# Chunk-selected attention feeding a softplus FFN: another start, a causal triangle by matmul, and a new order of all instructions

## The chip, the cores and the metric

The kernel runs on one core of one Trainium2 chip. The metric is the device time in microseconds of one execution. Engines are called by the profile's names: PE (TensorE, with PEld for its weight loads), DVE (VectorE), ACT (ScalarE), POOL (GpSimd) and SP (SyncE, which here only issues DMAs).

## The reference

q, k and v have 4 batches, 8 heads, 768 positions and 64 dimensions in f32. Each row of 768 keys is cut into 24 chunks of 32. For each query and chunk, an upper bound of the score is formed from the chunk's minimum and maximum of k; the six chunks with the highest bounds are kept, with a causal limit by chunk. Attention then runs over the kept chunks with the ordinary causal mask, and its output, 3072 tokens by 512, goes through an FFN with softplus.

```python
k_min = np.min(k_chunks, axis=3); k_max = np.max(k_chunks, axis=3)
ub = np.sum(np.maximum(q * k_min, q * k_max), axis=-1)      # per query and chunk
ub = np.where(causal, ub, -1e9)
top_chunks = np.argsort(ub, axis=-1)[..., -6:]
mask = (key's chunk is in top_chunks) & (pos[:, None] >= pos[None, :])
attn = softmax(np.where(mask, q @ k.T / 8, -1e9))
x = attn @ v                                                 # 3072 x 512
h = x @ w_in                                                 # 512 -> 2048
out = softplus(h) @ w_out                                    # 2048 -> 512
```

## The kernel before, in words

The work is cut into twelve blocks of 256 queries (4 batches of 3); block n is batch n // 3 and stretch n % 3. A block attends to the keys of its own stretch and of the earlier ones of its batch. Its four head pairs are handled one after the other.

For one block the steps are, by the names that the plan uses:

- Loads. `load` (line 330) issues two DMAs on POOL's queue for k, q or v, which turn f32 into bf16 on the way (line 339). k and q of block 0 come instead by `load_pairs` (line 345): four f32 halves on SP's queue into `xp` (line 352), each then cast into `io` by ACT or DVE. The FFN weights come in four chunks each on POOL's queue (`w_in`, line 376; `w_out`, line 383).
- k and q are transposed: by PE in blocks 0 to 2 (line 471), by a DMA transpose on SP's queue from block 3 on (line 475).
- DVE reduces k by chunk to maximum and negated minimum (`kx`, `kn`, lines 490 and 498) and copies them into a block-diagonal tile (`bd`). q is copied and split into its positive and negative part (`qc`, `qpn`, lines 547 to 551). PE forms the bounds (`ub`, line 570; line 574 adds the causal limit in blocks 0 to 2).
- DVE finds the sixth largest bound (`mx`, `raw`, lines 582 to 615). The mask, 32 rows a head, is transposed (`mT`, lines 627 and 633, or a DMA at line 636) and copied below q in the tiles `qa` and `qt` (`mc`). Block 0 does all this in two groups of two head pairs, the other blocks in one.
- The scores (`s`, lines 687 and 688) are one matmul over 96 or 128 rows: 64 of k and q, and 32 more, in which q's side holds the mask and k's side (`KA`, `KB`) holds one-hot rows that say to which chunk a key belongs and carry a large negative number. So a key of a chunk that is not selected gets a score that exp turns into 0.
- ACT takes exp into `pt` (line 695). In the two key tiles on the diagonal POOL then zeroes what lies above it (`af`, `affine_select`, line 705). PE multiplies by v with a column of ones (`av`, line 717), DVE divides (`nm`, lines 727 and 728), and the result is transposed into X (line 743 by PE and a copy in blocks 0 to 2 and the last; line 732 by DMA in the others).
- The FFN: `h` (line 791), exp (line 796) and ln(1 + x) (line 801) on ACT, `y` (line 816), a copy out of PSUM (line 822) and a store on SP's queue (line 827).

The one-hot rows are built in `ohb`: DVE fills it (line 270, one instruction for all three stretches), POOL cuts each stretch with three selects (lines 275 to 279), and SP's queue spreads them over the head pairs (`rows_of`, line 305), first the stretch of block 0, then the two others. Batches 1 and 3 use a second set of tiles, whose rows, like the loads of block 3, are gated on the last chunk of w_out.

None of this order is written out. `make_plan` lists operations with their engines (several where there is a choice), estimated costs, dependences and a key, a time by which they are wanted; `Plan.run` (line 136) passes urgencies back along the dependences and places one operation after the other by earliest start and urgency, with a model of the DMA queues (lines 179 to 188). The engines then run exactly in that order. All keys come from `PAR` (line 224): `a` holds the start of each block's scores, `prep` the lead of its preparation, `hlag` and `ylag` the lag of its FFN, `ahead` and `loads` the loads, `sizes` the number of buffers of each kind.

```python
o.due = min([o.key] + [s.due - dur for s in o.succ])          # line 146
lim = min(x[0] for x in v) + tol.get(e, 0)                    # line 169
x = min((x for x in v if x[0] <= lim), key=lambda x: (x[1].due, x[0], x[1].n))
```

At last `keep_awake` (line 837) fills the gaps that the plan leaves on PE in the first 45 us with matmuls of a zero tile (line 852). Their product is read by nobody.

Of the kernel before, what the change touches and what calls it, by code (L numbers as in the profile page):

```python
# [12 lines left out]
ALU = mybir.AluOpType  # L13
# [50 lines left out]

class Op:
    __slots__ = ("name", "alts", "fn", "deps", "gate", "after", "succ", "alloc", "touch", "key",
                 "rel", "packet", "port", "due", "wait", "eng", "start", "end", "done", "dma", "n", "at", "inst")


class Plan:  # L70
# [5 lines left out]
    def op(self, name, alts, fn, deps=(), alloc=(), touch=(), key=None, dma=None, gate=(), after=(), rel=0.0, packet=19.0, port=False):  # L76
        o = Op()
        o.rel, o.packet, o.port = round(rel), packet, port
# [50 lines left out]
    @staticmethod  # L129
    def home_at(pool, s, e):  # L130
        t = 0.0
        for q, x, dma in pool.ends[s]:
            t = max(t, x + (LANDED[e] if dma else 0 if q == e == "PE" else LAT[q].get(e, 150)))
        return t

    def run(self, par):
# [11 lines left out]
        ring, packet = {"SP": 0.0, "POOL": 0.0}, {"SP": 19.0, "POOL": 32.0}  # L148
# [3 lines left out]
        while ready:  # L152
# [26 lines left out]
            if o.dma:  # L179
                other = "SP" if e == "POOL" else "POOL"  # L180
                at = max(o.end + (650 if e == "SP" else 1150), ring[e], 2650.0)
                back, part = max(0.0, ring[other] - at), packet[other] / o.packet
                ring[e] = at + o.dma + min(o.dma * part, back)
                ring[other] += min(o.dma, back / part)
                packet[e] = o.packet
                o.done = ring[e] + (450 if o.packet < 100 else 1000)
                if e == "SP":
                    o.end = max(o.end, ring[e] - 3500)
            else:
                o.done = o.end  # L190
# [4 lines left out]
            for b in o.touch:  # L195
                b.left -= 1
                b.ends.append((e, o.done, bool(o.dma)))
# [22 lines left out]
def dve(n, rate=1.0):  # L220
    return n / (0.96 * rate) + 66


PAR = dict(
    dmat=3,
    dmaT=450,
    narrow=1,
    l0=1,
    over="soy",
    maskD=3,  # L230
    awake=(1.06, 45.0, 5.7),
    first=(64.42, 64.23, 29.03, 95.39),
    loads=((87.43, 130.15, 71.7), 19.14, (76.86, 12.06, 15.17), 41.22),
    tol={"PE": 0, "ACT": 0, "DVE": 0, "POOL": 2358, "SP": 0},
    alt=636,
    ohd=(229.35, 150.58),
    a=(-46.8, -33.92, -31.03, -0.05, 17.1, 24.77, 54.71, 88.7, 133.12, 175.62, 173.66, 255.42, 297.45, 469.8),
    prep=((77.31, -48.97, -81.43, 46.38), (-8.14, 24.92, -67.86, -43.68), (53.78, -16.07, -58.0, 11.26), (25.03, -41.37, -16.45, 11.23)),
    av=(-0.8, 4.76),
    ot=(12.12, 10.86),  # L240
    hlag=(8.7, 27.7, 34.1, -3.53, 34.9, 33.84, 33.54, 32.2, 25.36, -32.32, 54.03, 77.81),
    ylag=(7.32, 7.87, 25.64, 26.35, 28.67, 47.05, 47.88, 49.45, 10.02, 22.03, 47.36, 37.39),
    ahead=(3.4, 19.67, 10.64, 22.05, 12.72, 9.33, 70.63, 47.4, 103.95),
    sizes=dict(s=2, h=2, y=1, o=1, t=2, xf=2, xp=4, kT=2, io=8, kx=2, q=2, pn=2, ub=2, pt=4, osb=4, x=4, g=2, e=4, ysb=4, mT=2),
# [3 lines left out]
def make_plan(T, par):  # L248
# [19 lines left out]
    P.op("zero", [("DVE", 80)], lambda e: nc.vector.memset(T.zero, 0.0), key=-100000)  # L268
    ident = P.op("ident", [("POOL", 520)], lambda e: make_identity(nc, T.ident), key=1000)
    ohm = P.op("ohm", [("DVE", 700)], lambda e: nc.vector.memset(T.ohb, NEG), key=900)  # L270
    oh = []
    for k in range(NBLK):
# [8 lines left out]
        oh.append(P.op("oh", [("POOL", 1330)], f, [ohm], key=1500 + 6000 * k))  # L281
# [13 lines left out]
    chunk_rows = [P.op("c4", [("POOL", 900)], f4, [r4], key=3000)]  # L295
    mr0, bd0, kb0, vone, ohk = [], [], [], [], {}
# [11 lines left out]
    for k0, k1 in ((0, 1), (1, NBLK)):  # L308
        for h in range(2):
            o = P.op("ohk", [("SP", 450)], lambda e, k0=k0, k1=k1, h=h: rows_of(0, k0, k1, h), oh[k0:k1],  # L310
                     key=par["ohd"][k0] * 1e3, dma=300 * (k1 - k0))
            for k in range(k0, k1):
                ohk[0, k, h] = o
# [14 lines left out]
    def load(nm, n, when, gate=()):  # L328
# [6 lines left out]
        for t in range(NT):  # L335
# [4 lines left out]
                     gate=gate, key=key, rel=key - 2000 if n > 2 else 0.0, dma=950 if n < 3 else 2050, packet=32.0, **new)  # L340
            first = first or o
            ld[nm, n, t] = o

    def load_pairs(nm, n, when):
# [4 lines left out]
        for g in range(2):  # L349
# [4 lines left out]
                     key=1e3 * when[g], dma=950, packet=29.0, alloc=[st])  # L354
# [6 lines left out]
    def load_rows(nm, n, when):  # L361

        for t in range(NT):
            st = Buf(pool["xf"])
            d = P.op(f"ld {nm}{n}.{t}", [("SP", 560)], lambda e, t=t, st=st: nc.sync.dma_start(out=st.ap, in_=rows(nm, n, t)),
                     key=1e3 * (when + 0.3 * t), dma=1000, alloc=[st])
# [5 lines left out]
    def load_w_in(when):  # L372
        for c in range(4):
# [4 lines left out]
            w_in.append(P.op(f"w_in{c}", [("POOL", 800)], f, key=1e3 * (when + 0.4 * c), dma=2550, packet=173.0, after=w_in[-1:]))  # L378

    def load_w_out(when):  # L380
        for c in range(4):
# [4 lines left out]
            w_out.append(P.op(f"w_out{c}", [("POOL", 800)], f, key=1e3 * (when + 0.4 * c), dma=2550, packet=173.0,  # L386
# [5 lines left out]
    load_pairs("k", 0, (0.0, l0[0]))  # L392
    if par["l0"] < 2:
        load_pairs("q", 0, (l0[1], l0[2]))
    else:
        load("q", 0, l0[1])
# [4 lines left out]
    for nm, x in zip("kqv", l1):  # L401
        load(nm, 1, x)
    load_w_in(li)
    for nm, x in zip("kqv", l2):
        load(nm, 2, x)
    load_w_out(lo)
    for h in range(2):
        o = P.op("ohk", [("SP", 450)], lambda e, h=h: rows_of(1, 0, NBLK, h), oh, gate=[w_out[3]], key=40000, dma=900)
# [539 lines left out]
```

## Time and profile before

| | |
|---|---|
| three runs | 264.69, 266.26, 267.5 us; median 266.26 |
| the profiled execution | 266.59 us, of which the span of the trace is 264.8 us |
| granted PE clock over the span | 0.994 |
| busy | PE 255.0, PEld 197.2, DVE 142.5, ACT 211.0, POOL 110.8 us |
| line 852, the filler | 243 matmuls, 22.7 us of PE's 255.0 |
| longest line | 791, 91.8 us |
| DMA | 29.87 MB moved, 113 GB/s on average |

The page gives busy time by engine and in 40 slices of the span, the chain of work that ended last, and groups of instructions with their mean duration and the idle time ahead of them. Answers of the trace give the same for any stretch ("busy time by stretches": stretch, length, then busy time and number of instructions of PE, PEld, DVE, ACT and POOL, then the granted clock, the DMA share and GB/s) or for one line alone, and list instructions in order of time (start, duration, engine, line, operation, and in brackets how long the engine sat idle before it and what released it). Matmuls overlap in the pipeline, so that the sum of durations of a short one says less than the step from one start to the next.

### The profile page before, as it was taken

How to read it: one execution, taken by the hardware profiler on the slowest of the kernel's cores; microseconds unless marked ns; L12 is line 12 of the kernel's file. 1: busy time of each engine (PE TensorE's matmuls, PEld its weight loads, DVE VectorE, ACT ScalarE, POOL GpSimd, SP SyncE). 2: the span in 40 equal slices, each digit the busy share in tenths (PEclk: the TensorE clock that was granted, in tenths of full speed). 3: DMA queues.
4: the chain of work that ended last, by engine and by line, in shares of the span. 5: the costliest groups of instructions: out<-in, count | busy, mean ns of one | idle time of the engine just before them, and what ended most of it. 6: DMA issues, size and time to landing. Idle time of an engine off the chain costs nothing.

```text
span 264.8 us, 7039 instructions
## 1 busy us (share of the span) xinstructions
PE 255.0 (96%) x2750; PEld 197.2 (74%) x2779; DVE 142.5 (54%) x500; ACT 211.0 (80%) x372; POOL 110.8 (42%) x193
## 2 busy tenths in 40 slices
PE   8698999999999999999999999999999999999995
PEld 8698898768775677788678864777888756887744
DVE  6589961019789667447634596584582164221012
ACT  3589999988687879999687992699997885999900
POOL 8927878798318520543990263401110211310000
PEclk9799999999999999999999999999999999999999
DMA  7996999999999984699699969624440123001022
GB/s 162 161 189 90 181 196 231 155 139 190 149 136 173 132 119 89 115 129 100 73 173 150 117 88 174 173 54 120 45 82 0 42 72 99 10 2 42 0 79 79
DMA packets 114719, 29.87 MB, mean 113 GB/s; under 512 B 104544, under 2 KB 111712, under 8 KB 114688
## 3 DMA queue, kind: packets, MB, share of 16 engines
q0 software_dynamic: 74944, 13.11, 66.5%
q1 hardware_dynamic: 39744, 16.33, 33.0%
q8 instruction: 21, 0.34, 0.6%
q14 instruction: 10, 0.08, 0.1%
HBM read 27.26 MB, written 6.29 MB: 127 GB/s over the span
## 4 chain that ended last, share of the span: by engine, by line
PE 86%; DMA 5%; DVE 3%; ACT 3%; issue 1%; POOL 0%; DVEq 0%; POOLq 0%
PE ph L791 30%; PE py L816 17%; PE pt L816 9%; PE po L717 7%; PE ps L687 5%; PE py L852 4%; PE ps L688 4%; DMA io<-in_k_dram 3%; DMA x<-osb 3%; PE pt L687 2%; PE pt L688 1%; PE pt L570 1%; ACT g L801 1%; PE ph L816 1%; ACT e L796 1%
## 5 line engine op out<-in xcount | busy, mean ns | idle before, releaser
L791 PE MATMUL ph<-x,w_in_sb 128*128 128x256 bf16 x768 | 91.8, 272 | 0.0
L705 POOL TENSOR_SCALAR_AFFINE_SELECT pt<-pt 128x256 bf16<-128x256 bf16 x96 | 39.5, 419 | 112.6 <-ACT pt L695 112.1
L791 PEld LDWEIGHTS <-w_in_sb 128*128 128x128 bf16 x768 | 73.6, 98 | 11.5 <-DMA w_in_sb<-in_moe_w_in_dram 0.5
L695 ACT ACTIVATE pt<-ps 128x512 bf16<-128x512 f32 (+1 forms) x134 | 69.9, 564 | 9.4 <-PE ps L688 8.8
L796 ACT ACTIVATE e<-ph 128x512 f32<-128x512 f32 x96 | 56.3, 606 | 12.5 <-PE ph L791 11.8
L816 PEld LDWEIGHTS <-g 128*128 128x128 bf16 x400 | 37.4, 98 | 31.4 <-ACT g L801 0.5
L816 PE MATMUL py<-w_out_sb,g 128*128 128x512 bf16 x231 | 57.8, 379 | 1.5 <-ACT ysb L258 0.2
L801 ACT ACTIVATE g<-e 128x1024 bf16<-128x1024 f32 x48 | 51.1, 1072 | 1.0
L695 ACT ACTIVATE pt<-pt 128x512 bf16<-128x512 f32 (+1 forms) x58 | 32.4, 584 | 0.6 <-PE pt L688 0.6
L717 PEld LDWEIGHTS <-pt 128*128 128x128 bf16 x672 | 26.8, 97 | 5.1 <-issue 0.6
L259 DVE COPY ysb<-py 128x512 f32<-128x512 f32 x12 | 8.3, 691 | 36.9 <-PE py L816 36.9
L717 PE MATMUL po<-v,pt 128*128 128x65 bf16 x610 | 26.4, 193 | 0.3 <-DVE osb L728 0.3
L816 PE MATMUL pt<-w_out_sb,g 128*128 128x512 bf16 x108 | 26.2, 379 | 0.2
L727 DVE RECIPROCAL rec<-po 128x4 f32<-128x4 f32 x43 | 7.6, 178 | 34.9 <-PE po L717 34.6
L490 DVE TENSOR_REDUCE kx<-kT 128x32 bf16<-128x1024 bf16 x18 | 21.0, 1209 | 8.9 <-DMA kT<-io 8.9
L852 PE MATMUL py<-zero 128*128 128x128 bf16 x243 | 22.7, 245 | 1.1 <-DVE zero L268 1.1
L339 POOL DMA_DIRECT2D v<-in_v_dram x24 | 21.6, 905 | 3.8 <-DMA io<-in_q_dram 1.5
L339 POOL DMA_DIRECT2D io<-in_k_dram x22 | 20.0, 910 | 5.7 <-DMA w_in_sb<-in_moe_w_in_dram 2.2
L339 POOL DMA_DIRECT2D io<-in_q_dram x22 | 19.9, 910 | 0.7 <-PE ph L791 0.6
L728 DVE TENSOR_TENSOR osb<-po,rec 128x256 bf16<-128x256 f32 x43 | 18.2, 424 | 2.7 <-DMA x<-osb 1.3
L852 PEld LDWEIGHTS <-zero 128*128 128x128 bf16 x243 | 18.3, 111 | 1.3 <-DVE zero L268 1.1
L687 PE MATMUL ps<-qa,ka 96*128 96x256 bf16 x71 | 18.3, 273 | 0.7 <-DVE qa L259 0.7
(99 smaller groups left out, 302.5 us busy)
## 6 DMA issues: line engine op xcount, KB each, us to landing
out_dram<-ysb SPq DMA_DIRECT2D x23, 256.0 KB, 2.4
v<-in_v_dram POOLq DMA_DIRECT2D x24, 128.0 KB, 7.6
io<-in_k_dram POOLq DMA_DIRECT2D x22, 128.0 KB, 7.2
io<-in_q_dram POOLq DMA_DIRECT2D x22, 128.0 KB, 7.1
w_out_sb<-in_moe_w_out_dram POOLq DMA_DIRECT2D x4, 512.0 KB, 8.0
w_in_sb<-in_moe_w_in_dram POOLq DMA_DIRECT2D x4, 512.0 KB, 9.6
xp<-in_k_dram SPq DMA_DIRECT2D x2, 256.0 KB, 3.2
xp<-in_q_dram SPq DMA_DIRECT2D x2, 256.0 KB, 6.3
```

The source lines that it names most:

```text
L339: lambda e, t=t: nc.gpsimd.dma_start(out=into(nm, n, t), in_=rows(nm, n, t)),
L490: nc.vector.tensor_reduce(kx.ap[:, :, j].rearrange("d p (t c) -> d t p c", t=NT), kT.ap.rearrange("d p x -> d (p x)").rearrange("d (t p c ...
L687: nc.tensor.matmul(sp.ap[:, 0:QB], kk[0:nr, p, j * 128:(j + 1) * 128], qq, start=True, stop=True)
L695: lambda e, sp=sp, pt=pt, h=h, j=j, w=w: nc.scalar.activation(pt.ap[:, h, j:j + 2].rearrange("k j c -> k (j c)")[:, 0:w], sp.ap[:, 0:w], A ...
L705: nc.gpsimd.affine_select(out=d, in_=d, compare_op=ALU.is_ge, fill=0.0, base=0, channel_multiplier=-1, pattern=[[0, 2], [1, 128]])
L717: nc.tensor.matmul(o[:, u, h], pt.ap[:, h, j, c0:c0 + 128], T.V[i][:, j, 2 * p + h, :], start=(j == 0), stop=(j == t0 + u))
L728: nc.vector.tensor_tensor(osb.ap[0], o[:, :, :, 0:D], osb.ap[1].to_broadcast([128, NT, 2, D]), op=ALU.mult)
L791: nc.tensor.matmul(o[:, j], T.w_in[:, dt, ft * 128:(ft + 1) * 128], x.ap[:, dt], start=(dt == 0), stop=(dt == KDM - 1))
L796: lambda e, hb=hb, eb=eb, f2=f2: nc.scalar.activation(eb.ap[:, f2 * 512:(f2 + 1) * 512], hb.ap, ACT.Exp),
L801: lambda e, eb=eb, g=g, f4=f4: nc.scalar.activation(g.ap[:, f4 * 4:(f4 + 1) * 4].rearrange("f j c -> f (j c)"), eb.ap, ACT.Ln, bias=1.0),
L816: nc.tensor.matmul(yb.ap[:, 0:c1 - c0], g.ap[:, f, u * 128:(u + 1) * 128], T.w_out[:, f, c0:c1], start=(f == 0), stop=(f == KFF - 1))
L852: z.fn = lambda e: T.nc.tensor.matmul(T.pools["y"].homes[0][:, 0:128], T.zero, T.zero, start=True, stop=True)
```

## The change

The parts, and the diff cut to them:

- The fill of `ohb` is split, and the stretch of block 0 with its three selects has the most urgent key of all. The DMAs that spread these rows stand on SP's queue behind the four f32 halves. Loads on POOL's queue do not start before 3.3 us.
- The keys of all blocks are new. Block 0's scores lead block 1's by 29.7 us of key (12.9 before). In `first`, the halves of k and q of block 0 have new keys, k ahead.
- In blocks 0 and 1 the causal triangle is no longer cut by POOL out of `pt`. A tile `tri` holds 0 where a key may be seen and the large negative number where not; each score matmul on the diagonal leaves its accumulation open, and a matmul of `ident` and `tri` over 128 columns adds it.
- The planner's DMA model is replaced (class `Rings`: two queues that take turns, with a cost by packet, a time to land, and seven transfers at most on POOL's queue), all DMA costs are new, each operation's urgency can be moved by name (`tweak`, some 250 numbers), and the buffers change: io 8 to 7, q 2 to 3, pt 4 to 5, ysb 4 to 2.
- The filler matmuls have 512 columns where the gap allows it, 128 otherwise; the zero tile is 512 wide.
- `load_both` and the parameters `both` and `whole` are new, but with both=0 and l0=1 they are not used.

```diff
-        free = {"PE": 3000.0, ...}; ring, packet = ...
+        for o in topo:
+            o.due += 1e3 * par["tweak"].get(o.name, 0.0)
+        rings = Rings()
...
-    loads=((87.43, 130.15, 71.7), 19.14, (76.86, 12.06, 15.17), 41.22),
-    a=(-46.8, -33.92, -31.03, -0.05, 17.1, 24.77, 54.71, 88.7, 133.12, 175.62, 173.66, 255.42, 297.45, 469.8),
-    sizes=dict(..., io=8, kx=2, q=2, pn=2, ub=2, pt=4, osb=4, x=4, g=2, e=4, ysb=4, mT=2),
+    loads=((163.59, 151.05, 84.9), 87.8, (77.28, 67.14, 224.83), 15.3),
+    a=(-78.8, -49.07, -44.44, -42.37, 34.33, 59.68, 104.86, 105.55, 175.21, 244.28, 267.91, 364.15, 491.78, 674.36),
+    sizes=dict(..., io=7, kx=2, q=3, pn=2, ub=2, pt=5, osb=4, x=4, g=2, e=4, ysb=2, mT=2),
+    tweak={"w_out1": 39.87, "ld q0": 2.76, ...},
...
-    ohm = P.op("ohm", [("DVE", 700)], lambda e: nc.vector.memset(T.ohb, NEG), key=900)
+    ohm = [P.op(f"ohm{j}", [("DVE", 270 + 200 * j)], lambda e, j=j: nc.vector.memset(
+        T.ohb[:, QB:] if j else T.ohb[:, 0:QB], NEG), key=-900000 + 902000 * j) for j in range(2)]
...
-        oh.append(P.op("oh", [("POOL", 1330)], f, [ohm], key=1500 + 6000 * k))
+        oh.append(P.op(f"oh{k}", [("POOL", 1330)], f, [ohm[min(k, 1)]], key=1500 + 6000 * k if k else -900000))
...
+        t0_ = P.op("tri0", [("DVE", 100)], lambda e: nc.vector.memset(T.tri, 0.0), key=2000)
+        tri_ = [P.op("tri", [("POOL", 430)], lambda e: nc.gpsimd.affine_select(
+            out=T.tri, in_=T.tri, compare_op=ALU.is_ge, fill=NEG, base=0, channel_multiplier=-1, pattern=[[1, 128]]), [t0_], key=8000), ident]
...
-                     key=par["ohd"][k0] * 1e3, dma=300 * (k1 - k0))
+                     key=par["ohd"][k0] * 1e3 if k0 else -90000, dma=280 * (k1 - k0), packet=35.0 * (k1 - k0), land=2500.0 if k0 else 1000.0)
...
-  gate=gate, key=key, rel=key - 2000 if n > 2 else 0.0, dma=950 if n < 3 else 2050, packet=32.0, **new)
+  gate=gate, key=key, rel=key - 2000 if n > 2 else 3300.0 if par["l0"] == 1 else 0.0, dma=850, packet=13.3, land=(...), **new)
...
+                        add = last and tri
+                        for c0, c1, x in ((0, QB, qq), (QB, w, qq[:, 1] if last else qq)):
+                            jj = j + c0 // QB
+                            nc.tensor.matmul(sp.ap[:, c0:c1], kk[0:nr, p, jj * 128:(jj + 1) * 128], x, start=True, stop=not add)
+                            if add:
+                                nc.tensor.matmul(sp.ap[:, c0:c0 + 128], T.ident, T.tri, start=False, stop=True)
...
-                    if last:
+                    if last and not tri:
...
+        for w in (512, 128):
+            while True:
+                c = w / 1.2 if t < 1e3 * par["awake"][2] else mm(w)
```

More of the change, by code (lines that the diff above doesn't have):

```diff
@@ L179, in run @@
             if o.dma:
[L180 to L186, printed above, removed]
+                for x, y in rings.add(o, t - 2500.0):
+                    y += x.land
+                    if x is o or x.done != y:
+                        x.done = y
+                        for z in x.succ:
+                            z.at.clear()
                 if e == "SP":
-                    o.end = max(o.end, ring[e] - 3500)
+                    o.end = max(o.end, o.done - o.land - 3500)
             else:
@@ L238 @@
[L238 to L244, printed above, removed]
+    awake=(1.14, 45.0, 5.7),
@@ L837, in keep_awake @@
 def keep_awake(T, order, par):
-    fill, free = [], 1e3 * par["awake"][0]
+    fill, free = [], max(1e3 * par["awake"][0], 140 + next(o.end for o in order if o.name == "zero"))
     for o in order:
```

208 lines of the change are left out of this document (151 added, 57 removed).

## The prediction, made before the changed kernel ran

> **What bounds the kernel now.** I read the page first, then the busy time by stretches, then the same stretches for the filler matmuls alone (line 852, whose product nobody reads), then the timeline of the front, engine by engine.
>
> ```profile
> span 264.8 us, 7039 instructions
> ...
> PE 255.0 (96%) x2750; PEld 197.2 (74%) x2779; DVE 142.5 (54%) x500; ACT 211.0 (80%) x372; POOL 110.8 (42%) x193
> ```
>
> TensorE is busy 96% of the span, but part of that is filler. The next two answers separate it; each row is a stretch, its length, and busy time by engine (the second answer holds line 852 alone).
>
> ```profile
> 0.00:21.00 21.00, 17.61 (x228) 16.65 (x229) 14.97 (x43) 13.16 (x20) 15.23 (x31) 0.92 1.49 167
> 0.00:28.00 28.00, 23.90 (x347) 22.56 (x348) 21.64 (x73) 19.69 (x31) 20.86 (x41) 0.94 1.32 151
> 0.00:36.00 36.00, 31.48 (x476) 29.24 (x476) 29.14 (x106) 27.47 (x47) 27.32 (x53) 0.95 1.32 158
> ```
>
> ```profile
> 0.00:21.00 21.00, 13.83 (x140) 11.72 (x141) 0.92 1.49 167
> 0.00:28.00 28.00, 18.42 (x201) 15.36 (x201) 0.94 1.32 151
> 0.00:36.00 36.00, 21.51 (x234) 17.54 (x234) 0.95 1.32 158
> ```
>
> ```profile
> 60.00:240.00 180.00, 178.26 (x1900) 135.09 (x1923) 105.57 (x376) 149.89 (x270) 63.17 (x112) 1.00 0.93 103
> ```
>
> In the first 36 us TensorE does 31.48 - 21.51 = 9.97 us of work that counts, so 26.03 us are lost there. From 60 to 240 us it is busy 178.26 of 180: 1.74 us are left to win. The front is the only place where this change can gain much, and the long middle can almost only lose.
>
> What ends the front is the first FFN matmul (line 791), since FFN work is what keeps TensorE full afterwards. It needs X of block 0 and the first chunk of w_in.
>
> ```profile
> 36.06 1.03 PE L791 MATMUL ph<-x,w_in_sb 128*128 128x256 bf16 x8
> ```
>
> ```profile
> 34.64 0.64 ACT L258 COPY x<-pt 128x256 bf16<-128x256 bf16 x2
> ```
>
> I read the copies ending at 35.28 as the last of block 0's X, 0.8 us ahead of 36.06; call 36.06 T0. The question is how far T0 comes forward. For a T0 of 28 the same working gives a loss of 28 - (23.90 - 18.42) = 22.52 us, and for 21 it gives 21 - (17.61 - 13.83) = 17.22. So 8 us of T0 are worth 3.5 us: the work that was done before T0 must then be done behind it.
>
> **The change, part by part.** *One-hot rows.* Now they go out from 9.81 on, and the first lands 5.6 us later.
>
> ```profile
> ka<-ohb SPq DMA_DIRECT2D x1, 64.0 KB, 5.6
> ```
>
> ```profile
> 9.81 0.75 SPq L307 DMA_DIRECT2D ka<-ohb  x1
> ```
>
> ```profile
> 17.41 0.57 ACT L258 COPY qa<-ph 32x512 bf16<-32x512 bf16 x1
> ```
>
> ```profile
> 18.04 0.27 PE L687 MATMUL ps<-qa,ka 96*128 96x256 bf16 x1
> ...
> 18.20 0.27 PE L687 MATMUL ps<-qa,ka 96*128 96x256 bf16 x1
> ```
>
> The first of the two has landed at 15.4. The first scores start at 18.04, right behind the mask copy that ends at 17.98. So the rows are not the last to come, and moving them alone is worth 0. They become necessary once the mask is earlier: sent at about 4 and as slow as now they land near 10, soon enough for a mask at 10 or later. The moved selects (about 1.3 us on POOL) now stand ahead of the identity, which then is there at about 3.3 us; block 0's first k half is cast only at 4.46 (3.84 + 0.62, below), which hides it, and each us beyond that would be paid in full. On SP the rows stand behind the four halves, and nothing of the front is queued behind them there.
>
> *POOL's loads held until 3.3 us.* The q halves arrive late today because POOL's loads run beside them.
>
> ```profile
> 3.84 0.62 ACT L258 CAST io<-xp 128x512 bf16<-128x512 f32 x1 [1.75 <-DMA xp<-in_k_dram]
> 4.72 0.62 ACT L258 CAST io<-xp 128x512 bf16<-128x512 f32 x1 [0.26 <-DMA xp<-in_k_dram]
> 7.67 0.62 ACT L258 CAST io<-xp 128x512 bf16<-128x512 f32 x1 [2.33 <-DMA xp<-in_q_dram]
> ```
>
> ```profile
> 10.64 0.62 ACT L258 CAST io<-xp 128x512 bf16<-128x512 f32 x1
> ```
>
> ```profile
> 2.08 1.90 POOL L339 DMA_DIRECT2D io<-in_k_dram  x2
> ```
>
> ```profile
> DMA to landing us min/median/max: 3.0/4.6/6.8
> ```
>
> ```profile
> 9.50 0.62 PE L471 MATMUL ph<-ident,io 128*128 128x128 bf16 x8 [2.24 <-DMA io<-in_k_dram]
> ```
>
> The k halves land 0.88 us apart (3.84, 4.72), with little beside them. At that pace q would be there at 5.6 and 6.5. It came at 7.67, and the slowest half took 6.8 us, so about 9.2: 1.5 us a half, once POOL's loads (from 2.08) were in flight. With these held back some 1.2 us, about half of the delay goes: I take 7.3 for the second half (bounds 6.5 and 9.2). Besides, TensorE stood 2.24 us for k of block 1, which was placed ahead of block 0's q; the second q half was cast only at 10.64. By block 0's new lead (next paragraph) that order is turned round, so its cast moves from 10.64 to 7.3, 3.3 us.
>
> The Trainium skill, "DMA: Bandwidth & Descriptors", section "Queues, rings and completion order", says that each DMA engine goes round-robin between the queues it has work for, a packet at a time. This speaks against counting on 6.5: once POOL's loads start, near 5.3, the 1.2 us still to move would take 2.4, and q would land at 7.7, which makes T0 0.4 and the sum 0.3 us worse; the trace's 1.5 against 0.88 us a half agrees with it about.
>
> *Block 0 first.* The planner's keys put block 0 29.7 us ahead of block 1 (-78.8 and -49.07, in place of -46.8 and -33.92), so block 1's and 2's preparation stands behind block 0's. Now DVE does theirs while the second group of block 0 waits for its mask.
>
> ```profile
> 16.43 1.21 DVE L498 TENSOR_REDUCE kx<-ph 128x32 bf16<-128x1024 bf16 x1
> 18.10 2.36 DVE L498 TENSOR_REDUCE kx<-pt 128x32 bf16<-128x1024 bf16 x2 [0.45 <-PE pt L471]
> 20.37 1.05 DVE L259 COPY bd<-kx 64x64 bf16<-64x64 bf16 x4
> ```
>
> That is 1.21 + 2.36 + 1.05 = 4.6 us, which I take off T0 (bounds 0, if ACT sets the pace, and 4.6). ACT is the engine to be late next; it is 95% busy where block 0's exponentials run:
>
> ```profile
> 20.00:30.00 10.00, 9.47 (x17) 1.00 0.93 119
> ```
>
> *Fillers of 512 columns, a wider zero tile.* Their price is nothing while TensorE waits anyway. The granted clock matters more:
>
> ```profile
> 10.00:20.00 10.00, 9.93 (x150) 9.26 (x147) 7.17 (x24) 7.98 (x13) 5.17 (x8) 0.83 1.79 180
> ```
>
> ```profile
> 12.34 0.43 PE ph L471 x4
> ...
> 14.16 0.22 PE pt L471 x4
> ```
>
> These are rows of the chain of work that ended last. At 0.83 four transposes took 0.43 us of the chain, later 0.22. Without the 2.24 us stall I expect the full clock: three fours on block 0's path, 0.6 us.
>
> The Trainium skill, "TensorE: Matmul & The Clock Gate", section "Part 1: The HAM clock gate", says that the clock is halved after an idle window of about 3.4 us. By that the 2.24 us stall should have cost nothing and these 0.6 us would not be owed to it; the trace's 0.83 right behind the stall disagrees, so I keep them, and without them the sum is 0.5 us worse.
>
> *Triangle by matmul.* Sixteen selects leave POOL (425 ns each) and 32 matmuls of 128 columns are added. The step from 18.04 to 18.20, 0.16 us, holds 256 and 128 columns, so 128 columns cost about 0.055 us.
>
> ```profile
> L705 POOL TENSOR_SCALAR_AFFINE_SELECT pt<-pt 128x256 bf16<-128x256 bf16 x22 | 9.2, 425 | 8.0 <-ACT pt L695 7.8
> ```
>
> Block 0's sixteen replace filler: 0. Block 1's sixteen fall behind T0: 16 x 0.055 = 0.9 us where TensorE is the limit, 0 where ACT is; I take half, 0.45. Block 0's last pair is spared a select and its hand-over on the way from exp to A*V: 0.42 and an estimated 0.3, that is 0.7 us of T0. The tile itself costs a memset and one select, early, on engines with gaps.
>
> *Loads in another order.* Sizes from the page (a load of k or q is as large as one of v):
>
> ```profile
> v<-in_v_dram POOLq DMA_DIRECT2D x24, 128.0 KB, 7.6
> ...
> w_out_sb<-in_moe_w_out_dram POOLq DMA_DIRECT2D x4, 512.0 KB, 8.0
> w_in_sb<-in_moe_w_in_dram POOLq DMA_DIRECT2D x4, 512.0 KB, 9.6
> xp<-in_k_dram SPq DMA_DIRECT2D x2, 256.0 KB, 3.2
> ```
>
> Today w_in is issued from 27.55 on, behind three chunks of w_out, so it would hold T0 too. The new urgencies put w_out's second chunk far back (tweak +39.87) and I read w_in ahead of it. Ahead of w_in's first chunk I count four halves, the two one-hot rows, v, one chunk of w_out and k of block 1: 1024 + 128 + 256 + 512 + 256, with itself 2688 KB or 2.75 MB. At the 151 GB/s of the first 28 us that is 18 us, done near 21 (the first bytes land before 3.84); with q of block 1 and k, q of block 2 (0.79 MB) also ahead, near 26. I take it as hidden; the ends are 21 and 36.
>
> *Pools.* Two output buffers instead of four: a store lands in a few us and a block makes two, so 0, with an estimated 1 us if SP is stuck before a store. More score and q buffers only loosen. The middle's new order is priced at 0, with 1.74 us to win and the loss of the second rival.
>
> **The sum.** T0 = 36.06 - 3.3 - 4.6 - 0.6 - 0.7 = 26.9. The loss at 26.9, between the rows of 21 and 28, is 17.22 + (5.9 / 7) x 5.30 = 21.7 us, against 26.03: a gain of 4.3. Less 0.45 for the triangle, 3.9. The profiled execution took 266.59 us, so 262.7; it lies 0.33 above the median of 266.26, so I predict **262.4**.
>
> **Rivals.** *First, T0 goes as far as the loads let it*, to 21: a loss of 17.22, a gain of 8.8, less 0.45, 257.9. For it: DVE and ACT have room early (14.97 and 13.16 busy of 21). Against it: ACT is 95% busy from 20 to 30 us, and an earlier T0 gives it more to do there.
>
> *Second, slower: block 3 starves TensorE near 96 us.* Block 3's loads are gated on w_out's last chunk.
>
> ```profile
> 49.48 1.35 SPq L475 DMA_TRANSPOSE kT<-io  x1
> ```
>
> ```profile
> 39.00 1.77 POOL L339 DMA_DIRECT2D io<-in_k_dram  x2 [0.42 <-issue]
> ...
> 47.59 0.89 POOL L339 DMA_DIRECT2D io<-in_k_dram  x1 [2.18 <-DMA w_in_sb<-in_moe_w_in_dram]
> ```
>
> ```profile
> 94.36 0.42 DVE L728 TENSOR_TENSOR osb<-po,rec 128x256 bf16<-128x256 f32 x1 [1.28 <-DMA x<-osb]
> ```
>
> ```profile
> 96.54 3.66 PE L791 MATMUL ph<-x,w_in_sb 128*128 128x256 bf16 x32
> ```
>
> Today block 3's k is issued at 39.0. If w_out's last chunk takes w_in's place as the last weight, the gate opens near 47.6, 8.6 us later. X of block 3 goes by DMA transposes that free their buffers at 94.36, and its FFN starts at 96.54: 2.2 us of reserve. So TensorE would stand 8.6 - 2.2 = 6.4 us behind the before, whatever the front won: 266.3 + 6.4 = 272.7. It decides once block 3's k is issued more than 2.2 us late, past 41.2. Against it: k lands at 49 today because it queues behind all of w_in, and the bytes ahead of it stay the same.
>
> *Third, nothing comes of it*: T0 moves, and the same reserve of 2.2 us at 96, or an ACT already 95% busy, takes the lead back. What is left is between the triangle's 0.9 us and 2.2 us of gain: 264 to 267, 266 taken.
>
> **How the numbers follow.** The forecast has 0.46 (260 to 264.5), the first rival 0.14, the third 0.15, the second and its lesser forms 0.25. A measurement of this kernel tells about 1% (2.7 us) from no change. Faster takes the forecast but for 0.04 above 263.6, and the first rival: 0.56. Same takes that 0.04 and nearly all of the third, 0.18; slower 0.26. The range runs from 257.5, which holds most of the first rival, to 270, which holds the lesser forms of the second (3 to 4 of its 6.4 us): 257.5 to 270.
>
> **What would show it.** Right: q's last cast near 7.3 us and no stall of over 2 us ahead of block 0's q transposes; first scores near 14; the one-hot rows landed before them; the first FFN matmul near 27, with w_in's first chunk there before X; filler by then near 17 us against 21.51; 60 to 240 us still busy over 178. Wrong: a first FFN matmul that waits for w_in, a T0 near 36 with ACT or DVE full before it, or idle time of TensorE near 60 to 100 us that ends with a DMA transpose of block 3 or 4.

## The result and the profile after

The changed kernel takes 267.37 us (median of 20 runs) against 264.9 us for the one before (20 runs on the same chip). The ratio is 1.0084, with a 95% interval of 1.0059 to 1.0109: slower by a little under 1%, where 1.5% faster was forecast. Ratios leave out the few runs that lie over 1.5% above the fastest of their kernel, so they differ a little from the ratio of the medians.

The first lines of the page after, and its busy time by stretches (stretch, length, busy time of PE, PEld, DVE, ACT and POOL, granted clock, DMA share, GB/s). The third fence holds the filler, now line 966, alone.

```profile
span 264.8 us, 6769 instructions
...
PE 254.1 (96%) x2638; PEld 187.2 (71%) x2638; DVE 139.1 (53%) x495; ACT 213.7 (81%) x379; POOL 105.0 (40%) x178
```

```profile
0.00:29.00 29.00, 25.22 (x275) 16.70 (x276) 22.99 (x80) 22.75 (x41) 25.36 (x45) 1.00 1.53 172
0.00:36.00 36.00, 32.22 (x387) 23.25 (x388) 28.07 (x105) 29.58 (x54) 27.11 (x47) 1.00 1.47 178
...
60.00:240.00 180.00, 176.41 (x1806) 130.10 (x1805) 97.68 (x360) 151.13 (x269) 63.98 (x110) 1.00 0.92 100
```

```profile
0.00:29.00 29.00, 15.21 (x70) 6.42 (x70) 1.00 1.53 172
```

The front is better than forecast: by the prediction's own measure 36 - (32.22 - 15.21) = 18.99 us are lost in the first 36, against 26.03 (some 1.7 us of the difference are the triangle's own matmuls, which are new work). The middle is worse: 176.41 us busy from 60 to 240, against 178.26. The timeline of the front shows q's casts (ACT), the first scores, and the first FFN matmul, line 904:

```profile
6.70 0.62 ACT L332 CAST io<-xp 128x512 bf16<-128x512 f32 x1 [1.35 <-DMA xp<-in_q_dram]
7.56 0.62 ACT L332 CAST io<-xp 128x512 bf16<-128x512 f32 x1 [0.24 <-DMA xp<-in_q_dram]
```

```profile
16.06 0.27 PE L800 MATMUL ps<-qa,ka 96*128 96x256 bf16 x1
...
28.75 1.04 PE L904 MATMUL ph<-x,w_in_sb 128*128 128x256 bf16 x8
```

To see where the lead goes I use one curve. **Lost by t** is t less the PE work begun by then: each matmul that isn't filler, taken from its weight load in the trace, counted with the step of its shape at full clock (0.109 us for an FFN matmul of 256 columns, 0.216 for one of 512, 0.055 for 128 columns). The rows of the chain give such steps: 8 matmuls of line 904 take 0.87 us. After, there is 1.8 us more work to do, the triangle's 32 matmuls at 0.055.

| lost by, us | 40 | 60 | 75 | 95 | 155 | 200 | 255 |
|---|---|---|---|---|---|---|---|
| before | 24.5 | 25.3 | 25.3 | 26.0 | 25.9 | 26.2 | 26.4 |
| after | 18.5 | 19.1 | 19.2 | 21.3 | 21.6 | 24.5 | 24.8 |

At 60 us the new kernel leads by 6.2 us, 4.4 net of the triangle. It loses 2.1 us from 75 to 95 (before: 0.7) and 2.9 from 155 to 200 (before: 0.3), and the two profiled spans end equal. Both places can be seen in the timeline. First, 75 to 85 us, DVE and PE, and part of the chain that ended last:

```profile
78.44 0.60 DVE L333 COPY qa<-mT 32x512 bf16<-32x512 bf16 x2 [2.54 <-DMA mT<-mraw]
```

```profile
78.78 0.64 PE L800 MATMUL ps<-qa,ka 96*128 96x256 bf16 x4 [0.91 <-DVE qa L333]
```

```profile
72.16 9.51 DMA kT<-io
81.70 1.22 DVE kx L599
```

DVE waits 2.54 us for the DMA transpose of block 3's mask, PE waits for DVE, and a transpose of k takes 9.51 us of the chain. Second, 155 to 195 us, PE, and two DMA pieces of the chain:

```profile
162.02 0.71 PE L904 MATMUL ph<-x,w_in_sb 128*128 128x256 bf16 x5 [0.66 <-DMA x<-osb]
191.27 3.36 PE L904 MATMUL ph<-x,w_in_sb 128*128 128x256 bf16 x29 [0.73 <-DMA x<-osb]
```

```profile
154.44 7.53 DMA x<-osb
...
185.69 5.54 DMA x<-osb
```

A transpose of X waits in the transfers for 5 to 7.5 us, where the quickest takes 2.3 from issue to landing:

```profile
DMA to landing us min/median/max: 2.3/2.4/7.5
```

What else is in flight there are POOL's loads of block 10:

```profile
150.35 0.90 POOL L419 DMA_DIRECT2D io<-in_k_dram  x1
...
154.71 0.92 POOL L419 DMA_DIRECT2D v<-in_v_dram  x1
```

The planner has `rel=key - 2000` for them (line 420), so it places them near 160 us, behind the transposes. But the program holds only the order: POOL issues a load as soon as it comes to it, ten microseconds early.

Loads beside the transposes need not cost anything, though. The kernel before has the same `rel` (line 340), and there too six loads go out beside two transposes of block 7's X, which are issued at 158.84 and 161.30 us and take 5.4 and 5.2 us:

```profile
155.58 0.90 POOL L339 DMA_DIRECT2D io<-in_k_dram  x1 [0.39 <-issue]
...
160.31 0.91 POOL L339 DMA_DIRECT2D v<-in_v_dram  x1
```

But the last of these lands at 166.49 us and block 7's FFN starts at 168.51, so PE waits for nothing. In the new order it lands at 161.98, and the matmul that needs it starts at 162.02. What the new order lacks is the margin between a transfer and its use.

### The profile page after: what moved, and what is told of

Same layout as the page of the kernel before. It is cut to its first block, busy times and chain, and to the rows that moved or that the text cites. A ratio compares the mean times of both kernels' runs of the same rounds, so it can differ in the third digit from the quotient of the medians.

```text
span 264.8 us, 6769 instructions
## 1 busy us (share of the span) xinstructions
PE 254.1 (96%) x2638; PEld 187.2 (71%) x2638; DVE 139.1 (53%) x495; ACT 213.7 (81%) x379; POOL 105.0 (40%) x178
## 4 chain that ended last, share of the span: by engine, by line
PE 74%; DMA 10%; ACT 8%; DVE 4%; issue 1%; SPq 1%; ACTq 0%; DVEq 0%
PE ph L904 26%; PE py L929 18%; PE ps L800 9%; PE pt L929 8%; PE po L830 6%; DMA x<-osb 5%; DMA kT<-io 4%; PE pt L800 4%; DMA xp<-in_q_dram 2%; ACT qt L332 2%; ACT pt L808 2%; PE pt L830 1%; PE pt L679 1%; PE ph L929 1%; ACT e L909 1%
## 5 line engine op out<-in xcount | busy, mean ns | idle before, releaser
L808 ACT ACTIVATE pt<-ps 128x512 bf16<-128x512 f32 (+1 forms) x139 | 74.1, 579 | 12.6 <-PE ps L800 11.9
L818 POOL TENSOR_SCALAR_AFFINE_SELECT pt<-pt 128x256 bf16<-128x256 bf16 x80 | 32.5, 418 | 116.9 <-ACT pt L808 116.6
L909 ACT ACTIVATE e<-ph 128x512 f32<-128x512 f32 x96 | 58.1, 628 | 18.9 <-PE ph L904 17.9
L929 PE MATMUL py<-w_out_sb,g 128*128 128x512 bf16 x256 | 64.5, 379 | 0.1
L808 ACT ACTIVATE pt<-pt 128x384 bf16<-128x384 f32 (+1 forms) x53 | 30.0, 603 | 1.3 <-PE pt L800 1.1
L800 PE MATMUL ps<-qa,ka 96*128 96x256 bf16 (+1 forms) x144 | 24.0, 258 | 1.5 <-DVE qa L333 1.4
L800 PE MATMUL ps<-qt,kb 128*128 128x256 bf16 (+1 forms) x134 | 22.9, 259 | 1.0 <-ACT pt L808 0.8
L830 PE MATMUL po<-v,pt 128*128 128x65 bf16 x548 | 23.4, 193 | 0.5 <-DVE osb L841 0.5
L800 PEld LDWEIGHTS <-ka 96*128 96x128 bf16 x192 | 17.2, 97 | 7.3 <-issue 2.1
L419 POOL DMA_DIRECT2D v<-in_v_dram x24 | 21.7, 911 | 1.4 <-DMA io<-in_k_dram 0.6
L800 PEld LDWEIGHTS <-kb 128*128 128x128 bf16 x192 | 16.8, 97 | 6.6 <-issue 0.9
L333 DVE COPY ysb<-py 128x512 f32<-128x512 f32 x10 | 6.9, 691 | 24.0 <-PE py L929 24.0
```

What stands on the lines that cost most here:

```text
L333: return (nc.vector if e == "DVE" else nc.gpsimd).tensor_copy(dst, src)
L419: lambda e, t=t: nc.gpsimd.dma_start(out=into(nm, n, t), in_=rows(nm, n, t)),
L800: nc.tensor.matmul(sp.ap[:, c0:c1], kk[0:nr, p, jj * 128:(jj + 1) * 128], x, start=True, stop=not add)
L808: lambda e, sp=sp, pt=pt, h=h, j=j, w=w: nc.scalar.activation(pt.ap[:, h, j:j + 2].rearrange("k j c -> k (j c)")[:, 0:w], sp.ap[:, 0:w], A ...
L818: nc.gpsimd.affine_select(out=d, in_=d, compare_op=ALU.is_ge, fill=0.0, base=0, channel_multiplier=-1, pattern=[[0, 2], [1, 128]])
L830: nc.tensor.matmul(o[:, u, h], pt.ap[:, h, j, c0:c0 + 128], T.V[i][:, j, 2 * p + h, :], start=(j == 0), stop=(j == t0 + u))
```

## The experiments

Theory one: the front's lead is real, and the new order of the middle loses it at waits of its own, for transfers. Theory two, the rival: something with a pace of its own (ACT, the loads) takes back any lead in whatever order. Most kernels here hold the order of all instructions as a list that replaces the planner's choice, and the diffs show that list; their helper lines lie 104 or 105 higher (L437 or L438 for L333). Ratios are to the kernel before, run beside them; its medians were 266.1, 265.93, 264.88 and 265.65 us in the four sets.

**1 to 4: halves of the two orders, and a delay put in.**

```diff
 order of front_new_middle_old:
-[after: from 60 us]
+[after: to 60 us] + [before: all that is not yet placed]      # io 7, ysb 3
 order of front_old_middle_new: the other way round
```

```diff
 new_pe_delayed_3us, ahead of the first FFN matmul
+for _ in range(16): matmul(hb, zero[:, 0:128], zero)              # 512 columns
 old_pe_delayed_3us, at the same place in the old kernel
+for _ in range(62): matmul(hb[:, 0:128], zero, zero)              # 128 columns
```

> The operations that the new plan places in its first 60 us stand as the new plan has them; all others follow in the old kernel's order (with the triangle by matmul in blocks 0 and 1, and seven io and three ysb buffers, so that both orders fit). Theory one, the new middle is worse in itself, because its X and kT transposes stand too close ahead of what needs them: the front's lead of about 4.4 us (6.2 us less lost by 60 us, less 1.8 us of added triangle matmuls) is kept, so 4 us faster than before, about 261 us. Theory two, the middle hands back any lead, since the chain of blocks 3 and 4 over DMAs ends when it ends: within 1 us of before.

Measured: 266.69 us, 1.0038 (0.9998 to 1.0078). The time is the rival's number, but the curve tells another story. The new front is all there (19.0 us lost by 60), but just behind the seam PE waits for DVE's part of a block's preparation:

```profile
65.13 0.18 PE L784 MATMUL pt<-bd,qpos 128*128 128x16 bf16 x1 [1.46 <-DVE qpos L765]
```

DVE isn't overloaded there: from 60 to 75 us it is busy 10.73 us, before 12.89, after 11.04. So it's the order at the seam that costs. By 75 us 21.8 are lost, by 255 23.8: after the seam the old order loses only 2.0 us in 180. As the seam has its own loss, the time of this run doesn't decide between the theories.

> The mirror image: the old plan's first 60 us, then everything else in the new order, with the triangle by matmul. Theory one: before plus the triangle's 1.8 us plus the 4 to 6 us that the new middle loses, 270 to 273 us. Theory two: the later front takes up what the middle would have waited, so 266 to 268 us, no worse than the changed kernel.

Measured: 275.63 us, 1.0379 (1.0322 to 1.0437). Behind an old front the new middle loses 10.2 us (23.1 by 60, 33.3 by 255), more than the 4 to 6 that theory one expected: the mixture has losses of its own here too, such as 4.3 us from 95 to 155, where the new kernel loses 0.3. Some 1.7 us of these are clock, which in this execution was 0.79 from 110 to 118 us. That the new middle is the weak half agrees with theory one, but its size isn't to be read here.

> The changed kernel with sixteen matmuls of the zero tile, 512 columns each (about 3.45 us of TensorE), put ahead of the first FFN matmul; everything else, loads too, as it is. Theory one, the losses of the middle are placed by order and not by how far ahead TensorE is: 3 to 3.5 us slower than the changed kernel. Theory two, TensorE only arrives later at waits that end at the same time: within 1 us of the changed kernel.

> The control: the kernel before with the same 3.45 us of zero matmuls (62 of 128 columns) ahead of its first FFN matmul. If TensorE is its limit from there on, as its waits of under 2 us after 60 us say, 3 to 3.5 us slower than before. If it has slack that the profile hides, less.

Measured: 271.99 us, 1.0229 (1.0173 to 1.0286), and 268.33 us, 1.0100 (1.0064 to 1.0137). The delay of some 3.4 us costs 3.8 us over the new kernel, 2.7 over the old. With PE 3 us less ahead, the new kernel still loses at the same two places (22.5 to 23.8 from 75 to 95 us, 24.5 to 28.0 from 155 to 200). The first loss is 1.3 us in place of 2.1, so a part of it does go with the lead. But as a whole the lead isn't taken back because it is a lead: theory two, which had the delayed kernel within 1 us of the new one, falls.

**5 and 15: POOL's loads of blocks 10 and 11 held.** Only POOL's order is changed; block 11's loads move likewise behind `af10#1`. The kernel was run twice, on two chips, the second time as a control for runs 13 and 14.

```diff
 order on POOL:
 af7#6 af7#7
-ld k10.0  ld q10.0  ld v10.0  ld k10.1  ld q10.1  ld v10.1
 af8#0 af8#1
+ld k10.0  ld q10.0  ld v10.0  ld k10.1  ld q10.1  ld v10.1
 af8#2
```

> The changed kernel, with only POOL's order altered: the six loads of block 10 go behind the first two selects of block 8, those of block 11 behind the first two of block 10, which is about where the plan has them in time (160 and 193 us; on the chip they went at 150 and 184, since nothing holds them there). Theory: those loads meet the DMA transposes of X (one took 7.53 us where the plan has 3.19), and TensorE loses 1.9 us at 158 to 165 and 0.8 at 190 to 195; both go, so 2 to 2.7 us faster than the changed kernel. Rival: TensorE has run ahead of the chain and will wait at the next place; within 1 us of the changed kernel.

> The control: the new kernel with block 10's and 11's loads held and nothing else. Ratio to the old kernel 0.996, loss of about 1.3 to 1.8 us at 75 to 85 us, none at 155 to 195 us.

Measured: 264.71 us, 0.9959 (0.9930 to 0.9988), and 265.5 us, 0.9999 (0.9966 to 1.0033). Against the new kernel's 1.0084 that is 2.2 to 3.3 us won. In the trace of the second the loss from 155 to 200 us is 24.8 to 25.1, 0.3 us in place of 2.9, and the transpose of X that took 7.53 us takes 3.55. The second loss is explained: loads issued early, beside transposes of X that are needed as soon as they land.

**6: block 3's q transpose ahead of a store on SP.**

```diff
 order on SP:
 kD4 kD3
-st0#1
 qD3
+st0#1
 qD4
```

> The changed kernel with two instructions of SP's queue exchanged: the transpose of q of block 3 goes ahead of the second store of block 0, behind which it stood from 53.7 (data there) to 57.1 us. Theory: block 3's mask comes about 3 us earlier, DVE's 2.5 us wait for it at 76 us goes, and with it the 1.8 us that TensorE loses from 75 to 85: 1.5 us faster than the changed kernel. Rival: the next late one there, k of block 5, keeps the place; within 0.7 us.

Measured: 267.25 us, 1.0057 (1.0021 to 1.0092), about 0.7 us less than the new kernel, within the intervals of both. In the trace 20.5 us are lost by 90 (after: 21.0). At most a small part of the first loss.

**7 and 8: the triangle by select again, in the new order.**

```diff
-    tri=2,
+    tri=0,        # new_selects_back;  1 in new_triangle_block0_only
```

> The changed kernel's order with the triangle cut by POOL's selects again in blocks 0 and 1, each right behind its exponential, and no triangle matmuls. If the matmuls' price counts in full (32 x 0.055 us behind the start of the FFN or on the way to it), 1.8 us faster; if only block 1's, 0.9 us faster; if the selects' time and hand-over on block 0's way to X (0.7 us) and the loads that wait behind them on POOL cost more, slower by up to 2 us.

> As the run before, but block 0 keeps its triangle by matmul and only block 1 goes back to selects. If block 1's sixteen matmuls cost TensorE time and block 0's replace filler, 0.9 us faster than the changed kernel, and at least as fast as with selects in both blocks.

Measured: 271.02 us, 1.0196 (1.0143 to 1.0248), and 271.54 us, 1.0186 (1.0123 to 1.0248): both about 3 us slower than the new kernel. The forecast was 1.8 us faster to 2 us slower for the first and 0.9 us faster for the second, so both missed. POOL's timeline in the second shows one cause: block 1's selects now stand among the issues of w_out and of loads, which take 0.75 to 0.91 us each.

```profile
27.38 0.42 POOL L922 TENSOR_SCALAR_AFFINE_SELECT pt<-pt 128x256 bf16<-128x256 bf16 x1
27.73 1.50 POOL L581 DMA_DIRECT2D w_out_sb<-in_moe_w_out_dram  x2
29.23 0.43 POOL L922 TENSOR_SCALAR_AFFINE_SELECT pt<-pt 128x256 bf16<-128x256 bf16 x1
29.59 0.91 POOL L523 DMA_DIRECT2D v<-in_v_dram  x1
...
31.44 0.44 POOL L922 TENSOR_SCALAR_AFFINE_SELECT pt<-pt 128x256 bf16<-128x256 bf16 x1
```

A\*V of block 1 then starts at 32.17 us in place of 30.62, and 21.0 us are lost by 40 in place of 18.5. Later more is lost at 155 to 200 us too (23.8 to 29.4), where the loads of block 10 meet the transposes; 1.7 us of that are clock, 0.72 from 164 to 170 us in this execution. In this order the matmuls are worth more than they cost.

**9 and 10: the two mends together, and the gate of block 3.**

```diff
 new_loads_held_and_q3_first: the diffs of 5 and 6
 new_loads_held_block3_gate_early: the diff of 5, and
-            load(nm, n, ..., gate=[w_out[3]] if n < 4 else ())
+            load(nm, n, ..., gate=[w_out[2]] if n < 4 else ())
```

> The new kernel with both mends at once: block 10's and 11's loads held on POOL's queue behind later selects, and block 3's q transpose ahead of a store on SP's queue. Theory: the two losses are separate waits, so the two gains (3.3 us and 0.7 us against the new kernel) add: ratio to the old kernel 0.993 or less, about 263.5 us. Rival: time won at 80 us is spent again at a later wait, and nothing is added to the loads alone: ratio 0.996.

Measured: 264.0 us, 0.9964 (0.9936 to 0.9992). The rival's number; the interval doesn't quite exclude that a little is added. The busy time from 155 to 200 us, first of the kernel before, then after, then of this one:

```profile
155.00:200.00 45.00, 44.68 (x443) 32.00 (x447) 30.86 (x102) 36.22 (x65) 12.20 (x24) 1.00 0.73 101
```

```profile
155.00:200.00 45.00, 43.03 (x441) 32.14 (x439) 22.63 (x82) 35.19 (x68) 14.07 (x27) 1.00 0.94 100
```

```profile
155.00:200.00 45.00, 45.00 (x458) 33.70 (x457) 23.11 (x82) 37.33 (x73) 18.08 (x31) 1.00 0.79 93
```

PE is full there again. But from 75 to 95 us it still loses 1.8 us (19.2 to 21.0), so q's transpose isn't the cause of the first loss.

> The new kernel with block 10's and 11's loads held, and block 3's loads released by w_out's third chunk in place of its fourth. Theory (the bytes ahead set when k of block 3 lands, not its issue): the loads are issued some us before 44 us, but land near 50 us as they do now, and the time stays that of the loads held alone, ratio 0.996 (0.994 to 0.998). Rival, the second rival of the prediction (the late gate is what costs): k of block 3 lands 4 us or more earlier, DVE's wait for its mask goes, and 1 to 1.8 us are won: ratio 0.990 to 0.992.

Measured: 264.9 us, 0.9998 (0.9970 to 1.0027): no gain. The loads of block 3's k go out 3.75 us earlier (first fence; 44.56 in the new kernel) and land 2.5 to 3 us earlier by the trace (near 48 us), yet DVE waits as long for the mask:

```profile
40.81 1.75 POOL L523 DMA_DIRECT2D io<-in_k_dram  x2 [6.82 <-ACT qt L436]
```

```profile
79.30 0.60 DVE L437 COPY qa<-mT 32x512 bf16<-32x512 bf16 x2 [2.98 <-DMA mT<-mraw]
```

**11 and 12: the triangle by matmul in the old order, and its control.** The lists are the old kernel's own order, with its buffer counts; in 12 the selects of blocks 0 and 1 are left out and the tile `tri` is made early.

```diff
 old_order_old_triangle:        tri=0
 old_order_triangle_by_matmul:  tri=2
                               on POOL
 c4#0
+tri#0
-af0#0 ... af0#7  af1#0 ... af1#7
                               on DVE
+tri0#0
```

> The old kernel's order and buffer counts run through the new code, selects on POOL in blocks 0 and 1, with the new code's split one-hot fill and its wide fillers. Both theories: nothing of the path is changed, ratio 0.997 to 1.003. It is the control for the next run.

> As the control, but with the triangle of blocks 0 and 1 by matmul, in the old order. The prediction: block 0's matmuls replace filler, block 1's cost 0 to 0.9 us, and the select's hand-over saves 0.7 us: together within 0.5 us of the control. Rival (the selects are on the path in any order, as the 3 us of the run with the selects back suggest): 2 to 3 us faster than the control. Third possibility, all 32 matmuls at full price and no hand-over saved: 1.8 us slower.

Measured: 265.93 us, 1.0031 (1.0000 to 1.0061), and 265.95 us, 1.0035 (1.0010 to 1.0061). The triangle alone is worth nothing either way: 22.4 us are lost by 60 in place of 24.2, and that 1.8 us is what its matmuls take. The control itself is 0 to 0.6% above the old kernel; which part of the new code (wide fillers, the split fill) costs that isn't shown.

**13 and 14: what keeps block 3's mask.** Both have the diff of 5.

```diff
 order on SP, both:
 st1#0
-qD5
 mD3
+qD5
 kD5
 order on POOL, the second only:
 ld k6.1  ld q6.1
-ld v6.0  ld v6.1
 af3#0 ... af3#7
+ld v6.0  ld v6.1
```

> The new kernel with block 10's and 11's loads held, and block 3's mask transpose ahead of block 5's q transpose on SP's queue. Theory one (its place on the queue costs): it is issued near 68.8 us in place of 70.2, lands near 77 in place of 78.4, as in the old kernel, and 0.9 to 1.4 us of the loss at 75 to 85 us go: about 1.1 us faster than the control. Theory two (the transfers in flight set it): it lands near 78 all the same, and the time stays within 0.5 us of the control.

Measured: 264.05 us, 0.9970 (0.9942 to 0.9998); the control beside it 0.9999, so some 0.8 us won, though the two intervals overlap. The mask lands at 75.9 us by the trace, and DVE doesn't wait for it. But DVE then waits for the next two transposes, and PE for DVE:

```profile
78.84 0.52 DVE L764 TENSOR_SCALAR qpos<-qt 128x1024 bf16<-128x1024 bf16 x1 [1.62 <-DMA qt<-io]
...
81.59 1.22 DVE L703 TENSOR_REDUCE kx<-kT 128x32 bf16<-128x1024 bf16 x1 [1.36 <-DMA kT<-io]
```

```profile
83.42 0.34 PE L934 MATMUL po<-v,pt 128*128 128x65 bf16 x6 [1.50 <-DVE osb L945]
```

19.1 us are lost by 80 in place of 20.4, but 20.8 by 85, nearly as many as before the mend: the wait has moved on by one transpose.

> As the run before, and block 6's two loads of v held on POOL's queue behind block 3's last select, so that about 0.5 MB less stands beside the mask's transpose. Theory one: nothing beyond the run before. Theory two: the mask lands another 1 to 3 us earlier, near 75 to 76 us, DVE no longer waits for it, and the loss at 75 to 85 us falls under 0.4 us: 1.5 to 2 us faster than the control, about 262.5 us.

Measured: 262.38 us, 0.9897 (0.9854 to 0.9939), the best here: 1.0% faster than the old kernel, 1.9% than the new. With two loads fewer in flight the transposes behind the mask come earlier, and the waits shrink:

```profile
76.70 0.60 DVE L437 COPY qa<-mT 32x512 bf16<-32x512 bf16 x2 [0.71 <-DMA mT<-mraw]
78.36 0.43 DVE L764 TENSOR_SCALAR qpos<-qt 128x1024 bf16<-128x1024 bf16 x1 [0.42 <-DMA qt<-io]
80.05 1.22 DVE L703 TENSOR_REDUCE kx<-kT 128x32 bf16<-128x1024 bf16 x1 [0.39 <-DMA kT<-io]
```

Theory two of this pair holds for the time but not for the mask: it lands at 76.7 us, no earlier than in the run before. What comes earlier with the fewer loads are the transposes of q and k behind it, landing at 78.33 and 80.03 us for 78.81 and 81.57. 19.5 us are lost by 85 (after: 20.9).

The curves together:

| lost by, us | 40 | 60 | 75 | 95 | 155 | 200 | 255 |
|---|---|---|---|---|---|---|---|
| old order, triangle by matmul | 22.1 | 22.4 | 22.2 | 22.5 | 22.7 | 23.0 | 23.5 |
| after | 18.5 | 19.1 | 19.2 | 21.3 | 21.6 | 24.5 | 24.8 |
| loads held, q of block 3 first | 18.3 | 19.0 | 19.2 | 21.0 | 21.6 | 21.9 | 21.8 |
| loads held, mask 3 first, v of block 6 late | 18.5 | 19.2 | 19.3 | 19.7 | 20.7 | 21.1 | 21.0 |

The first two rows do the same work. The new order wins 3.3 us by 60 and loses 5.7 from there to 255, the old one 1.1: a balance of 1.3 us to the bad. The times say the same (1.0084 less 1.0035, or 1.3 us).

## Why the prediction was wrong

The step that failed is "The middle's new order is priced at 0, with 1.74 us to win and the loss of the second rival." The prediction gave no reason why a new order should cost nothing. It costs about 4.6 us (5.7 against 1.1), at two waits for DMA transposes on SP's queue that run beside POOL's loads and are needed as soon as they land. The front's gain came nearly as forecast and was paid back there; idle time of PE at 60 to 100 us that ends, here by way of DVE, with a DMA transpose of block 3 is one of the prediction's own signs of being wrong. In numbers: 3.9 us of gain were forecast and 2.2 of loss came (1.0084), 6.1 apart. By the single traces 4.6 of these are the middle, 0.6 the front (22.4 less 19.1 is 3.3 us won by 60 us, for 3.9), and some 0.8 what the control of run 11 lies above the old kernel. Point by point:

- **One-hot rows, 0.** They were issued at 2.97 and 3.75 us and landed by 8.0, long ahead of the scores. Right, though the selects didn't come ahead of the identity, as the prediction had it, but behind it (1.53 us and 1.08). No run shows their share alone.
- **POOL's loads held.** q's second half is cast at 7.56 us; 7.3 was forecast. Right, and the wait of 2.24 us for block 1's k ahead of block 0's q is gone.
- **Block 0 first, 4.6 us, with the select's 0.7.** From the first scores to T0 it took 18.0 us before and 12.7 after: as a sum the 5.3 came in full, though no run takes the two terms apart. What fell short lies ahead of the scores, which start at 16.06, not 14. PE transposes block 0's masks at 12.49 and 13.71, but ACT copies the first only from 15.17 on. It has no idle time from 7.56 us until the scores, and three of its instructions there, 1024 wide where block 0's are 512, are a later block's q:

```profile
12.10 1.01 ACT L332 COPY qt<-ph 128x1024 bf16<-128x1024 bf16 x1
13.14 1.06 ACT L656 ACTIVATE qpos<-qt 128x1024 bf16<-128x1024 bf16 x1
14.11 1.04 ACT L656 ACTIVATE qneg<-qt 128x1024 bf16<-128x1024 bf16 x1
```

  So ACT set the pace up to the scores, and T0 is 28.75 for 26.9. Yet the loss in the first 36 us fell by 7.0 us for 4.3, since PE had done more by then: 25.22 - 15.21 = 10.0 us of work that counts by 29 us, where the sum had 26.9 - 21.7 = 5.2 by T0. A T0 put too early and work counted too low made up for each other, so that the front's gain came near the forecast is in part luck.
- **The clock, 0.6 us, and the base.** The profile that I argued from had a stretch of reduced clock (the row of before, then of after):

```profile
10.00:15.00 5.00, 5.00 (x73) 5.00 (x69) 3.27 (x12) 3.38 (x6) 4.86 (x8) 0.66 2.25 165
```

```profile
10.00:15.00 5.00, 4.69 (x62) 3.19 (x61) 2.56 (x17) 4.88 (x7) 4.56 (x8) 1.00 1.43 185
```

  0.66 over 5 us is some 3.4 us at half speed. Of the 100 runs of the old kernel beside the experiments, 69 had a mean clock of 0.998 or more, with a median of 264.9 us, and 29 one of 0.990 to 0.997, with 266.5. So the profiled 266.59 us was an execution with such a stretch, and the base of 266.26, from three runs, was about 1.4 us too high; part of the 6.2 us between the two curves is that, and a full clock was no gain of the change. The Trainium skill, "TensorE: Matmul & The Clock Gate", section "Part 1: The HAM clock gate", says that the window behind the clock is free-running, so that the same kernel has a different number of slow matmuls at its start from run to run. These runs agree in kind, for a stretch inside the front: the kernel is the same in all, and most show no loss of clock. I had tied it to the stall; whether it takes an idle time at all isn't shown.
- **The triangle, 0.7 us of T0 less 0.45.** In the old order it is 0 against its control, in line with the terms. In the new order the selects would cost some 3 us, in part because they stand behind POOL's own issues; the rest isn't shown. The prediction didn't see that the new order depends on it.
- **The loads, hidden.** w_in's first chunk landed at 25.9 us, X's last copy began at 26.85. Right.
- **Pools, 0.** Runs 9, 13 and 14 win 3 to 5 us back with the new buffer counts, so these aren't what costs that. No run changes them alone.
- **The second rival.** Its condition came true (block 3's k was issued at 44.56, past 41.2), its price of 6.4 us did not: k landed at 50.0 to 51.1 against 48.6 to 49.4, for the reason given against it (the same bytes ahead), and run 10 shows that even this did not matter. It named the right block and the right kind of wait at 75 to 95 us, for another cause.
- **The third rival**, the lead taken back, 264 to 267 us, is nearest to the result; but neither ACT nor the reserve at 96 us took it.

The missed thing could have been asked of the plan: in both kernels the loads have a release time that only the planner keeps, and the middle's transposes share the transfers with those loads. The old order leaves room for that (2.0 us at block 7's X), the new one doesn't (0.04). The loss at 75 to 95 us is shown by runs 13 and 14 to hang on the order of the transposes and the loads in flight; 0.4 us that run 14 still loses there, and 1 us that it loses from 95 to 155, stay open.

## What to carry to other kernels

A front's gain counts only if the middle has nothing that slips. Where a planner orders transfers by time but the chip keeps only their order, compare the planned and the real issue of each load; a load that goes out early can delay the short transfers beside it, and whether that costs anything hangs on the margin between a transfer and its use. Before a profile is taken as the base, look at its granted clock and at how its time stands to many runs.

## What the runs showed of the hardware

In these traces a DMA transpose takes longer the more is in flight beside it: those of X land 2.3 us after issue when little moves, and 5 to 7.5 us with six loads just issued; those of q, k and the mask issued from 57 to 77 us, with POOL's loads in flight throughout, take 6.5 to 9.6 us. In the kernel before, those issued from 49 to 71 us take 8.1 to 10.9 us, and PE loses 0.7 us from 75 to 95 us all the same. The Trainium skill, "DMA: Bandwidth & Descriptors", section "Queues, rings and completion order", says that each DMA engine takes turns between its queues packet by packet; the trace agrees in kind, since SP's transposes are stretched by POOL's loads without ever standing behind them on a queue.

Stretches of half clock came at no fixed place: 10 us in the profile of before, 112 us in that of run 2 (0.79 from 110 to 118 us), 165 us in that of run 8 (0.72 from 164 to 170). At some 3.4 us of half speed each is worth about 1.7 us, so a loss in one trace has to be read with the granted clock beside it.
